# One Fourier-filter and gated-convolution kernel, one core: the hand-made planner gets a new order, laid out with a rule for eight transfers in flight

## The chip, the core and the metric

The kernel runs on one core of a Trainium2 chip. The time is that of one execution on the device, in microseconds (us); the kernel before takes 857.64 us (median of three runs, 857.32 to 858.21). One further execution was profiled; all views below are of that one.

## The reference

Everything is float32. A real Fourier transform along the sequence, a complex 256 x 256 matrix on the channels with a soft threshold, the transform back, and then a gated convolution:

```python
X = rfft(x, axis=1)                       # x: 8 batches x 3200 positions x 256 channels
Yr = Xr @ w_r - Xi @ w_i + b_r            # soft threshold, lam = 0.01, on Yr and on Yi
Yi = Xr @ w_i + Xi @ w_r + b_i
y = irfft(Yr + 1j * Yi, n=3200)
gate = sigmoid(causal_conv_5_taps(y, conv_w))
out = (gate * (y @ w_val)) @ w_out
```

## The kernel before, in words

The transform of length 3200 is split into 50 x 64, so that all of it is matrix products on TensorE (PE). A batch goes through three phases, and between them its data passes through DRAM, because the transform needs it turned round.

- **p1(b, u)**, u = 0 to 7: a tile of x (0.41 MB, four transfers, two of them of 48 rows and two of 2 rows; u = 0 has six) is loaded; PE multiplies it (L594, L599, L601) into a PSUM buffer of the tag ps_2, ACT copies one half out (L607) and VectorE (DVE) folds it twice (L613) into an SBUF tile s of the tag s1; then it is stored to a_dram (L554, and for u = 0 also four small transfers of L631).
- **p2(b, d)**, d = 0 to 6: a part of a_dram is loaded into a (two transfers, L650); PE does **s2** (L668, for d = 6 L660) into ps_2; ACT and DVE split the result into high and low parts xs (L709, L713, L716, L717, L720, L721). For each of its two units PE does **mixsum** (six matmuls, L786), DVE adds the bias (L788), and PE does **mix** (twelve matmuls, L782; the 13th unit is L772 and L773) into a buffer y_ps of which there are two, which ACT has seeded with the bias (L764). ACT and DVE make the threshold (L794, L796), PE does **s1i** (L737, last L731), ACT copies it out (L747) and it is stored to z_dram (L753).
- **p3(b, k)**, k = 0 to 7: zl is loaded from z_dram, PE does **s2i** (L848), ACT copies to y_sb (L852), DVE and ACT do the convolution and the sigmoid (L896, L899, L909), PE the two products v_ps and o_ps (L882, and L878 in the last blocks), DVE the gate (L933), ACT copies out (L958) and the result is stored (L960).

The tag ps_2 has three buffers, s1 two, x three, a two; batch 0's p1 borrows further SBUF tiles (tag by u: `("s1", "g_hl", "xs")[u % 3]`). A buffer is used again when its last reader is done, in the order in which pieces are emitted.

The weights w_val and w_out come as float64 words, and DVE turns each into float32 in thirteen instructions that stand behind each other in its row (L430, L436: the **conversion block**).

The order of all this is not left to a scheduler. The class `Plan` gets each piece with a due time `at`, an engine and a guessed duration, and `order()` plays them through: at each step it takes the engine whose next piece can begin first, and of the pieces that can begin within SLACK of that the one with the smallest due time. The kernel emits the instructions in that order, and each engine and each queue works its own row strictly in it. The due times are sums of the loop counters and of the table `O`. Transfers are nearly all issued from one queue, SP, in the planned order; the planner models them with one wire of `WIRE` bytes per ns, a completion time of `LANDED` ns, and a limit on the `BACKLOG`. Where it expects PE to stand still, it puts matmuls of zeros in (`fill`, L363 `zeros`).

Of the kernel before, what the change touches and what calls it, by code (L numbers as in the profile page):

```python
# [104 lines left out]
class Plan:  # L105
# [11 lines left out]
    def add(self, at, engine, busy, fn, uses=(), sets=(), new=None, delay=None, mode="r", kb=0, chain=None, extra=0):  # L117
        n = len(self.pieces)
        before = set()
        for key in uses:  # L120
            before |= set(self.writers.get(key, ()))
        for key in sets:
            before |= set(self.readers.get(key, ())) | set(self.writers.get(key, ()))
        for key in uses:
            self.readers.setdefault(key, []).append(n)
        for key in sets:
            self.writers[key], self.readers[key] = [n], []
        p = dict(n=n, at=at, engine=engine, busy=busy, fn=fn, before=before, new=new or {}, mode=mode, kb=kb, extra=extra,
                 tiles={key[:2] for key in (*uses, *sets)}, delay=busy + LAND[engine] if delay is None else delay)
        p["behind"] = {self.last[chain]} if chain in self.last else set()  # L130
        if chain:
            self.last[chain] = n
        self.pieces.append(p)
        return n

    def order(self):
        pieces = self.pieces
        for p in pieces:
            for tile_ in p["new"]:
                self.opened[tile_] = p["n"]  # L140
        users = {t: 0 for t in self.opened}
        after, follow = ([[] for _ in pieces] for _ in range(2))
        for p in pieces:
            opener = ({self.opened[t] for t in p["tiles"] if t in self.opened} | p["behind"]) - p["before"] - {p["n"]}
            for n in opener:
                follow[n].append(p["n"])
            p["left"] = len(p["before"]) + len(opener)
            p["ready"] = 0.0
            for n in p["before"]:
                after[n].append(p["n"])  # L150
            for t in p["tiles"]:
                if t in users:
                    users[t] += 1
        ends = {t: 0.0 for t in users}
        rows = {tag: [] for tag in self.slots}
        engines = sorted({p["engine"] for p in pieces})
        waiting = {e: [] for e in engines}
        for p in pieces:
            if not p["left"]:
                waiting[p["engine"]].append(p)  # L160
        free = {e: 0.0 for e in engines}
        mode, wire = "r", 0.0
        done = []

        def opens(p):
            at, ahead = 0.0, {}
            for tag in p["new"].values():
                row = rows[tag]
                n = len(row) + ahead.get(tag, 0)
                ahead[tag] = ahead.get(tag, 0) + 1  # L170
                if n >= self.slots[tag]:
                    old = row[n - self.slots[tag]]
                    if users[old]:
                        return None
                    at = max(at, ends[old])
            return at

        while len(done) < len(pieces):
            best = None
            for e in engines:  # L180
                could = []
                for p in waiting[e]:
                    at = opens(p)
                    if at is not None:
                        could.append((max(free[e], p["ready"], at, wire - BACKLOG if p["kb"] else 0.0), p))
                if not could:
                    continue
                first = min(c[0] for c in could)
                near = [c for c in could if c[0] <= first + SLACK[e]]

                lone = e == "PE" and sum(c[1]["mode"] == "q" for c in near) < 2
                start, p = min(near, key=lambda c: (c[1]["at"] + (0.0 if e != "PE" or c[1]["mode"] != "q" else -O["together"] if mode == "q"
                                                                   else O["hold"] if lone else 0.0), c[0]))
                if best is None or start < best[0]:
                    best = start, p
            assert best is not None, "no piece can begin"
            start, p = best
            e = p["engine"]
            waiting[e].remove(p)
            busy, delay = p["busy"], p["delay"]  # L200
            if e == "PE":
                slow = max([f for until, f in CLOCK if start < until], default=1.0)
                busy, delay = busy * slow, delay * slow
                to = SWITCH.get(mode + p["mode"], 0)
                busy, delay, mode = busy + to, delay + to, p["mode"]
            if p["kb"]:
                wire = max(wire, start + 800) + p["kb"] * 1024 / WIRE
                delay = wire - start + LANDED + p["extra"]
            free[e] = start + busy
            end = start + delay  # L210
            p["start"], p["end"], p["open"] = start, end, opens(p)
            done.append(p)
            for t, tag in p["new"].items():
                rows[tag].append(t)
            for t in p["tiles"]:
                if t in users:
                    users[t] -= 1
                    ends[t] = max(ends[t], end)
            for n, at in [(n, end) for n in after[p["n"]]] + [(n, start) for n in follow[p["n"]]]:
                q = pieces[n]  # L220
                q["left"] -= 1
                if q["engine"] == "PE" != e and at == end:
                    at += WEIGHTS
                q["ready"] = max(q["ready"], at)
                if not q["left"]:
                    waiting[q["engine"]].append(q)
        return done
# [42 lines left out]
WEIGHTS = 130  # L270
CLOCK = ((28000, 1.6), (45000, 1.2))
FILL = 36000, 200000
WIRE = 250
BACKLOG = 5000
LANDED = 2500


def dve(n, copy=False):
# [3 lines left out]
def act(n, kind="copy"):  # L282
# [6 lines left out]
NW = (NT - 1) * N1 + P  # L289
NG = NT // 2 * P + P  # L290
T = float(NU)
O = {'spread': -91.8948,
     'hold': 1.0724,
     'together': 1.2701,
     'later': -3.6572,
     'load_x': 9.9589,
     'p1': 0.1254,
     'p1_step': 1.2361,
     'load_a': -5.3199,
     's2': -1.7149,  # L300
     's1i': 1.553,
     'p3': 1.0966,
     'load_z': -28.9681,
     'y': 11.7985,
     'conv': 25.53,
     'val': 6.1049,
     'gate': -22.7084,
     'project': 7.8156,
     'late_val': 6.023,
     'late_out': 14.484,  # L310
     'turn': -55.8644,
     'pre': -4.984,
     'mix_sum': -1.4205,
     'p1_1': -7.3343,
     'load_x_1': -7.2435,
     'p1_2': -1.5627,
     'p3_0': 0.9988}
WARM = 2, 1, 1, 1, 8
SLOTS = {"x": 3, "zl": 3, "y_hl": 2, "s1": 2, "a": 2, "xs": 2, "sx": 1, "xz": 1, "tp": 3, "zst": 2,
         "acc": 2, "g_hl": 2, "o": 2, "ps_y": 2, "ps_2": 3, "a_dram": 2, "z_dram": 2}  # L320
# [6 lines left out]
def fourier_filter_then_gated_conv(ctx: ExitStack, tc: tile.TileContext, x, w_r, w_i, b_r, b_i,  # L327
# [5 lines left out]
    dram = ctx.enter_context(tc.tile_pool(name="dram", bufs=2, space=bass.MemoryType.DRAM))  # L333
    LATE_VAL, LATE_OUT = set(LATE[int(O["late_val"]):]), set(LATE[int(O["late_out"]):])
    plan = Plan(SLOTS)
    add = plan.add
# [214 lines left out]
    def by_rows(eng, out, in_, rows):  # L551

        for lo, hi in rows:
            eng.dma_start(out=out[lo:hi], in_=in_[lo:hi])  # L554
# [4 lines left out]
    STORED = []  # L559
# [4 lines left out]
    def p1(b, u, at):  # L564
# [8 lines left out]
        def load(h):  # L573
            xt = room(kx, x_tag, 4 * D) if h in (0, None) else tl[kx]
            src = x[b].rearrange("(n m) c -> n (m c)", m=N1)
            for g in range(NH) if h is None else (h,):
                eng = QUEUES[g][1] if early and u < BOTH else nc.sync
                lo = (N1 - 3 - 4 * u if g else 4 * u) * D
                n = 3 * D if g and u == 0 else 4 * D
                by_rows(eng, xt[half(g), 0:n], src[:, lo:lo + n], rows)  # L580
                if n < 4 * D:
                    by_rows(eng, xt[half(g), n:], src[:, NM * D:(NM + 1) * D], rows)
        if early:
            for h in range(NH):
                add(-100 + u, QUEUES[h][0] if u < BOTH else "SP", 650, lambda h=h: load(h), (), [kx + (h,)], None if h else {kx: x_tag}, kb=200)
        else:
            add(at + O["load_x"] + O["load_x_1"] * (b == 1), "SP", 1300, lambda: load(None), STORED if b == 1 else (),
                [kx + (0,), kx + (1,)], {kx: x_tag}, kb=400, chain="x")

        def products():  # L590
# [25 lines left out]
        busy = 2 * dve(D) if u == 0 else dve(512)  # L616
# [405 lines left out]
    for b in range(B):  # L1022
# [12 lines left out]
        start = (b + 1) * T + O["p3"] + O.get(f"p3_{b}", 0.0)  # L1035
# [40 lines left out]
```

## Time and profile before

| | |
|---|---|
| runs | 857.32, 857.64, 858.21 us |
| profiled execution | 859.73 us, of which the span from the first to the last instruction is 857.8 us |
| PE, matmuls | 821.0 us busy, 96% of the span, mean granted clock 0.973 |
| DVE | 736.2 us busy, 86% |
| ACT | 593.7 us busy, 69% |
| DMA | 162.27 MB, mean 189 GB/s |

Busy time of PE counts matmuls from start to end, and they overlap; a row of the timeline gives start, time taken, engine, line and tiles, and the distance from one row's start to the next is what a piece really costs PE. PEclk is the share of TensorE's clock that was granted. SPq is the queue that issues transfers: its rows are the issues, not the transfers.

### The profile page before, as it was taken

The numbers are of one execution on the slowest core, as the hardware profiler recorded it, in microseconds if no ns is written. First come the engines' busy times: TensorE is split into PE (matmuls) and PEld (weight loads), VectorE is DVE, ScalarE is ACT, GpSimd is POOL, SyncE is SP. The second block draws the span as 40 slices with busy tenths as digits, with TensorE's granted clock in tenths as the row PEclk, the third lists the DMA queues.
The fourth block names the chain that finished last, engine by engine and source line by source line (L and its number), as shares of the span: only waits on it lengthen the run. The fifth ranks groups of instructions, "written<-read, shape, count | busy, mean of one in ns | idle before, by whom it ended". The sixth has DMA issues, their size and how long they took to land.

```text
span 857.8 us, 23810 instructions
## 1 busy us (share of the span) xinstructions
PE 821.0 (96%) x9866; PEld 700.7 (82%) x9866; DVE 736.2 (86%) x1006; ACT 593.7 (69%) x903; POOL 4.5 (1%) x12
## 2 busy tenths in 40 slices
PE   8878867999999999999999999999999999999997
PEld 2456656889888988889988989899888999998874
DVE  3345679799998999899989998999989998998795
ACT  2234635778777786778777886878777787776753
POOL 0000000000000000000000000000001000000000
PEclk7888979999999999999999999999999999999999
DMA  6688889867886569776796759876895576225422
GB/s 169 182 190 224 246 214 250 228 179 191 209 234 185 165 180 258 203 204 174 224 245 195 192 175 248 206 206 187 231 234 158 157 200 193 71 83 173 133 76 96
DMA packets 125909, 162.27 MB, mean 189 GB/s; under 512 B 12528, under 2 KB 100234, under 8 KB 125802
## 3 DMA queue, kind: packets, MB, share of 16 engines
q1 hardware_dynamic: 125598, 160.34, 68.1%
q8 instruction: 78, 1.28, 0.7%
q10 hardware_dynamic: 204, 0.41, 0.2%
q14 instruction: 29, 0.24, 0.1%
HBM read 82.06 MB, written 78.64 MB: 187 GB/s over the span
## 4 chain that ended last, share of the span: by engine, by line
PE 69%; DVE 13%; DMA 9%; ACT 4%; SPq 3%; issue 2%; DVEq 0%; ACTq 0%
PE o_ps L882 13%; PE y_ps L782 12%; PE v_ps L882 11%; PE y_p L848 10%; PE y_ps L786 6%; DMA x<-in_x 4%; PE p L594 4%; PE s L668 4%; PE z_ps L737 4%; DVE acc L899 4%; PE v_ps L878 2%; SPq L554 2%; DMA zl<-z_dram 1%; DVE acc L933 1%; DVE gated L390 1%
## 5 line engine op out<-in xcount | busy, mean ns | idle before, releaser
L899 DVE SCALAR_TENSOR_TENSOR acc<-y_sb,cw_sb,acc 128x800 f32<-128x800 f32 x256 | 263.0, 1047 | 16.1 <-ACT acc L896 15.6
L782 PEld LDWEIGHTS y_ps<-w_sb,xs 128*128 128x128 f32 x1152 | 144.3, 191 | 28.4 <-DVE y_ps L788 12.4
L782 PE MATMUL y_ps<-w_sb,xs 128*128 128x256 f32 x1152 | 156.3, 286 | 11.1 <-DVE y_ps L788 11.0
L882 PE MATMUL o_ps<-gated,wo_sb 128*128 128x400 f32 x744 | 150.8, 349 | 0.8 <-DVE gated L390 0.8
L882 PEld LDWEIGHTS o_ps<-gated,wo_sb 128*128 128x128 f32 x744 | 134.6, 188 | 4.1 <-DVE gated L390 1.1
L882 PE MATMUL v_ps<-y_hl,wv_sb 128*128 128x400 f32 x648 | 128.4, 346 | 0.5 <-DVE s L613 0.5
L882 PEld LDWEIGHTS v_ps<-y_hl,wv_sb 128*128 128x128 f32 x648 | 115.4, 188 | 1.1 <-PE y_ps L786 0.7
L613 DVE TENSOR_TENSOR s<-p,s 128x512 f32<-128x512 f32 (+2 forms) x144 | 89.3, 626 | 27.5 <-ACT s L607 16.4
L848 PEld LDWEIGHTS y_p<-g_sb,zl 100*64 100x64 f32 x2048 | 89.1, 137 | 11.7 <-ACT y_ps L764 3.5
L848 PE MATMUL y_p<-g_sb,zl 100*64 100x100 f32 x2048 | 97.4, 251 | 0.7 <-DMA zl<-z_dram 0.5
L786 PE MATMUL y_ps<-w_sb,xs 128*128 128x256 f32 x576 | 90.0, 293 | 7.6 <-ACT y_ps L764 7.6
L786 PEld LDWEIGHTS y_ps<-w_sb,xs 128*128 128x128 f32 x576 | 79.3, 194 | 20.9 <-ACT y_ps L764 9.0
L794 ACT ACTIVATE tp<-y_ps,nlam 128x512 f32<-128x512 f32 (+1 forms) x104 | 70.0, 674 | 25.1 <-PE y_ps L782 25.1
L388 ACT CAST gated<-acc 128x800 fp32r<-128x800 f32 x62 | 53.3, 859 | 30.7 <-DVE acc L933 30.5
L601 PE MATMUL p<-x,f_sb 50*64 50x512 f32 x240 | 72.2, 654 | 1.7 <-DMA x<-in_x 1.7
L933 DVE TENSOR_TENSOR acc<-v_ps,acc 128x800 f32<-128x800 f32 x64 | 62.9, 984 | 11.4 <-PE v_ps L878 5.5
L796 DVE SCALAR_TENSOR_TENSOR tp<-y_ps,tp 128x512 f32<-128x512 f32 (+1 forms) x104 | 68.6, 661 | 4.1 <-ACT tp L794 4.0
L594 PE MATMUL p<-x,f_sb 50*64 50x512 f32 x256 | 71.6, 647 | 0.1
L668 PEld LDWEIGHTS s<-f_sb,a 64*64 64x64 f32 x3072 | 53.7, 137 | 19.5 <-issue 11.6
L909 ACT ACTIVATE acc<-acc 128x800 f32<-128x800 f32 x64 | 55.8, 878 | 16.3 <-DVE acc L899 16.0
L958 ACT COPY o<-o_ps 128x800 f32<-128x800 f32 x63 | 51.8, 822 | 21.3 <-PE o_ps L882 15.8
L716 DVE TENSOR_TENSOR sx<-s,sx 128x512 f32<-128x512 f32 x48 | 33.0, 688 | 38.2 <-ACT xs L713 37.2
(92 smaller groups left out, 1031.3 us busy)
## 6 DMA issues: line engine op xcount, KB each, us to landing
out<-o SPq DMA_DIRECT2D x126, 200.0 KB
a<-a_dram SPq DMA_DIRECT2D x96, 256.0 KB
z_dram<-z_t SPq DMA_DIRECT2D x48, 512.0 KB
zl<-z_dram SPq DMA_DIRECT2D x64, 384.0 KB
a_dram<-s SPq DMA_DIRECT2D x120, 192.0 KB
x<-in_x SPq DMA_DIRECT2D x119, 192.0 KB
a_dram<-s SPq DMA_DIRECT2D x120, 8.0 KB
x<-in_x SPq DMA_DIRECT2D x119, 8.0 KB
```

The lines of the kernel that those rows point to most:

```text
L594: nc.tensor.matmul(p[k * HP:(k + 1) * HP, 0, :], f1_sb[half(0), 0:HP], xt[half(0), k * 512:(k + 1) * 512], start=True, stop=True)
L601: nc.tensor.matmul(dst, f1_sb[half(1), 0:HP], back[:, 2 * k:2 * k + 2, :], start=True, stop=True)
L613: nc.vector.tensor_tensor(out=st()[lo:hi, h, n], in0=tl[kp][lo:hi, 0, n], in1=st()[lo:hi, 1, n], op=(ALU.add, ALU.subtract)[h])
L668: nc.tensor.matmul(p[e * HP:(e + 1) * HP, h, c, t, :], tl[ka][rows, t, c * P + e * HP:c * P + (e + 1) * HP], f2_sb[rows, (4 * d + t) * N1: ...
L782: nc.tensor.matmul(p[:, 1 - r, :], xm(hx, c, r, i), w_sb[:, m, hw, c, :], start=False, stop=k == 5, skip_group_check=True)
L786: nc.tensor.matmul(tl[ky][:, 0], sm(hx, c, i), w_sb[:, 0, hw, c, :], start=False, stop=k == 5, skip_group_check=True)
L794: nc.scalar.activation(out=buffer(kt, "tp", [P, 2, D])[:, 0:n], in_=tl[ky][:, 0:n], func=AF.Relu, bias=nlam)
L796: add(at + 0.2, "DVE", dve(n * D), lambda: nc.vector.scalar_tensor_tensor(out=tl[kt][:, 0:n], in0=tl[ky][:, 0:n], scalar=LAM, in1=tl[kt][: ...
L848: nc.tensor.matmul(dst[e * HP:(e + 1) * HP], zt[0:Q, m, c * P + e * HP:c * P + (e + 1) * HP], g, start=True, stop=True)
L882: nc.tensor.matmul(p[:, e, 0:TB], w[:, hw, c, e * P:(e + 1) * P], src(hy, c), start=n == 0, stop=n == 5)
L899: nc.vector.scalar_tensor_tensor(out=acc(c), in0=wide(c, j), scalar=cw_sb[:, c, j:j + 1], in1=acc(c), op0=ALU.mult, op1=ALU.add)
L933: add(at + O["gate"], "DVE", dve(2 * TB), lambda: nc.vector.tensor_tensor(out=part(), in0=by_half(tl[kv][:, :, 0:TB]), in1=part(), op=ALU. ...
```

## The change

The planner's model gets one more rule: it keeps the landing times of the last eight transfers of each of two groups (those issued from POOL, and the others), and a transfer may not begin before the eighth one ahead of it has landed. `WIRE` goes from 250 to 260 and `LANDED` from 2500 to 2200, all values of `O` are new, and the first x tiles of batch 1 no longer wait until batch 0's p1 results are stored (`STORED`). No tile, no instruction's shape and no number of buffers changes; PE's real matmuls are the same in number. Only the filling zeros go from 26 to 71 instructions. `SOFT` is set and used nowhere.

```diff
+        lanes, turn = {e: [0.0] * 8 for e in (False, True)}, {False: 0, True: 0}
+        def lane(p):
+            row, at = lanes[p["engine"] == "POOL"], turn[p["engine"] == "POOL"]
+            return max([row[(at + j) % 8] - 350 * j for j in range(lanes_of(p))], default=0.0)
...
-                        could.append((max(free[e], p["ready"], at, wire - BACKLOG if p["kb"] else 0.0), p))
+                        could.append((max(free[e], p["ready"], at, max(wire - BACKLOG, lane(p)) if p["kb"] else 0.0), p))
...
+                n = lanes_of(p)
+                for j in range(n):
+                    lanes[e == "POOL"][turn[e == "POOL"] % 8] = start + delay - p["kb"] * 1024 / WIRE * (n - 1 - j) / n
+                    turn[e == "POOL"] += 1
...
-WIRE = 250
+WIRE = 260
-LANDED = 2500
+LANDED = 2200
+def lanes_of(p):
+    return max(1, round(p["busy"] / (520 if p["engine"] == "POOL" else 360))) if p["kb"] else 0
...
-     'load_x': 9.9589,
+     'load_x': 40.9418,
...
-     'load_x_1': -7.2435,
+     'load_x_1': -69.2562,
...
-            add(at + O["load_x"] + O["load_x_1"] * (b == 1), "SP", 1300, lambda: load(None), STORED if b == 1 else (),
+            add(at + O["load_x"] + O["load_x_1"] * (b == 1), "SP", 1300, lambda: load(None), (),
```

In the changed kernel every line of the body stands 14 lines lower (L668 is L682 and so on); the text keeps the numbers of before.

**SP, where batch 0's second phase begins.** Before, the first parts of a (L650) are loaded right behind batch 0's last store (s_254), and batch 1's x follows between them:

```order
L554 DMA a_dram<-s_254 48x2x512
L554 DMA a_dram<-s_254 2x2x512
L490 DMA g_sb<-in_g 128x256
L650 DMA a<-a_dram 64x4x256 x2
L554 DMA x<-in_x 48x1024
L554 DMA x<-in_x 2x1024
L554 DMA x<-in_x 48x768
```

In the changed kernel three x tiles of batch 1 stand ahead of batch 0's stores and two more behind them, and only then come the loads of a, for d = 0 and d = 1 together (L664):

```order
L568 DMA x<-in_x 48x1024
L568 DMA x<-in_x 2x1024
L504 DMA g_sb<-in_g 128x256
L499 DMA f_sb<-in_f 128x256
L664 DMA a<-a_dram 64x4x256 x4
L568 DMA x<-in_x 48x1024
L568 DMA x<-in_x 2x1024
```

The first load of a moves from the 73rd transfer of this queue, with 6.98 MB ahead of it, to the 96th, with 9.16 MB ahead. Behind it now stand batch 1's last three x tiles (twelve transfers), and only then the stores of batch 1's first p1 results (s_306, s_337, s_408); a for d = 2 comes behind those.

**PE, at the first s2 (s_317 before, s_461 now).** Before:

```order
L987 MATMUL warm<-idle 128x512 x8
L363 MATMUL s_317<-zero_sb 128x128 x15
L668 MATMUL s_317<-f_sb,a 64x64 x32
L594 MATMUL p_374<-x,f_sb 64x512 x2
L599 MATMUL p_374<-x,f_sb 64x256 x2
L601 MATMUL p_374<-x,f_sb 64x512
L363 MATMUL p_396<-zero_sb 128x128 x9
```

Now (p_355 and p_380 are p1 of batch 1, u = 3 and 4):

```order
L608 MATMUL p_355<-x,f_sb 64x512 x2
L615 MATMUL p_355<-x,f_sb 64x512 x2
L377 MATMUL y_ps<-zero_sb 128x128 x2
L608 MATMUL p_380<-x,f_sb 64x512 x2
L615 MATMUL p_380<-x,f_sb 64x512 x2
L377 MATMUL y_ps<-zero_sb 128x128 x49
L682 MATMUL s_461<-f_sb,a 64x64 x32
L377 MATMUL y_ps<-zero_sb 128x128 x8
L682 MATMUL s_520<-f_sb,a 64x64 x32
```

Thirteen p1 pieces stand ahead of the first s2 where eight stood, and 49 zeros directly ahead of it.

**DVE and PE, at the first conversion block.** On DVE the block (st_894 is the loaded w_val, st_1086 the result) stood behind four folds of a p1:

```order
L788 TENSOR_TENSOR y_ps<-y_ps,bias_sb 128x256
L613 TENSOR_TENSOR s_1064<-p_1042,s_1064 128x256
L613 TENSOR_TENSOR s_1064<-p_1042,s_1064 64x256
L613 TENSOR_TENSOR s_1064<-p_1042,s_1064 128x256
L613 TENSOR_TENSOR s_1064<-p_1042,s_1064 64x256
L430 TENSOR_SCALAR st_1086<-st_894 128x512
```

It now stands behind the 11th bias addition and two small pieces of the 13th unit:

```order
L802 TENSOR_TENSOR y_ps<-y_ps,bias_sb 128x256
L710 CAST xz<-xs 128x512
L711 MEMSET xz 128x8
L444 TENSOR_SCALAR st_1161<-st_1030 128x512
L444 TENSOR_SCALAR st_1161<-st_1161 128x512 x3
```

PE, at the matmuls that wait for the bias addition behind the block: before, the mixsum (L786) of that unit is followed at once by its mix (L782):

```order
L599 MATMUL p_1042<-x,f_sb 64x256 x2
L601 MATMUL p_1042<-x,f_sb 64x512
L782 MATMUL y_ps<-w_sb,xs 128x256 x12
L786 MATMUL y_ps<-w_sb,xs 128x256 x6
L782 MATMUL y_ps<-w_sb,xs 128x256 x12
```

Now another mix and a whole s2 stand between them:

```order
L751 MATMUL z_ps<-tp,g_sb 64x256 x8
L800 MATMUL y_ps<-w_sb,xs 128x256 x6
L796 MATMUL y_ps<-w_sb,xs 128x256 x12
L682 MATMUL s_1185<-f_sb,a 64x64 x32
L796 MATMUL y_ps<-w_sb,xs 128x256 x12
```

More of the change, by code (lines that the diff above doesn't have):

```diff
@@ L272 @@
 FILL = 36000, 200000
-WIRE = 250
+WIRE = 260
 BACKLOG = 5000
-LANDED = 2500
+LANDED = 2200
+SOFT = 1500
+def lanes_of(p):
+    return max(1, round(p["busy"] / (520 if p["engine"] == "POOL" else 360))) if p["kb"] else 0
 def dve(n, copy=False):
@@ L291 @@
 T = float(NU)
[L292 to L295, printed above, removed]
-     'load_x': 9.9589,
[L297 to L308, printed above, removed]
+O = {'spread': -86.7866,
+     'hold': 0.9457,
+     'together': 1.3242,
+     'later': 3.7239,
+     'load_x': 40.9418,
+     'p1': -3.5894,
+     'p1_step': 1.5365,
+     'load_a': 23.6096,
+     's2': -1.5367,
+     's1i': 0.9416,
+     'p3': 7.1139,
+     'load_z': -8.9038,
+     'y': 3.7564,
+     'conv': 75.8192,
+     'val': 4.1041,
+     'gate': -19.9155,
+     'project': 5.84,
      'late_val': 6.023,
      'late_out': 14.484,
[L311 to L314, printed above, removed]
-     'load_x_1': -7.2435,
-     'p1_2': -1.5627,
-     'p3_0': 0.9988}
+     'turn': -33.3683,
+     'pre': -59.4674,
+     'mix_sum': -1.3262,
+     'p1_1': 1.8084,
+     'load_x_1': -69.2562,
+     'p1_2': 1.7884,
+     'p3_0': -1.6866}
 WARM = 2, 1, 1, 1, 8
```

## The prediction

> **What bounds the kernel now.** I read the stretches first (start and end in us; busy time and count of PE, of its weight loads, of DVE, ACT and POOL; granted clock, DMA share, GB/s), to see where PE loses time at all.
>
> ```profile
> 20.00:40.00 20.00, 20.00 (x83) 10.02 (x82) 9.19 (x15) 5.72 (x11) 0.00 (x0) 0.85 0.72 197
> 40.00:60.00 20.00, 15.01 (x208) 10.77 (x208) 7.06 (x13) 5.54 (x10) 0.00 (x0) 0.83 0.84 186
> 180.00:220.00 40.00, 40.00 (x496) 36.01 (x494) 38.03 (x54) 30.00 (x48) 0.00 (x0) 1.00 0.58 158
> 220.00:260.00 40.00, 38.39 (x512) 34.30 (x512) 39.56 (x52) 30.67 (x48) 0.00 (x0) 1.00 0.88 229
> 420.00:460.00 40.00, 40.00 (x557) 35.33 (x559) 35.66 (x47) 29.42 (x46) 0.00 (x0) 1.00 0.86 234
> 780.00:820.00 40.00, 39.83 (x376) 32.58 (x375) 32.46 (x35) 23.86 (x33) 0.00 (x0) 1.00 0.50 147
> ```
>
> From 180 to 820 us PE stands still for hardly 2 us, at full clock. In that stretch no order can win anything: it can only add switches or waits. What an order can change lies ahead of 180 us. The waits of PE up to 180 us (who, for whom, total, times, longest), and one of those after it, which lies in the last blocks:
>
> ```profile
> PE y_ps L782 <- DVE y_ps L788: 11.0, 3, 7.6
> PE y_ps L786 <- ACT y_ps L764: 6.6, 3, 4.5
> PE s L668 <- DMA a<-a_dram: 5.0, 2, 4.2
> PE s L668 <- DMA f_sb<-in_f: 2.5, 1, 2.5
> ...
> PE o_ps L882 <- DVE gated L390: 0.8, 1, 0.8
> ```
>
> So the question is how much PE work is done when the first s2i begins, and when that is. Pieces of PE cost, start to start where nothing waits:
>
> ```profile
> 160.53 0.95 PE L786 MATMUL y_ps<-w_sb,xs 128*128 128x256 f32 x6
> 161.32 1.52 PE L782 MATMUL y_ps<-w_sb,xs 128*128 128x256 f32 x12
> 162.77 0.65 PE L594 MATMUL p<-x,f_sb 50*64 50x512 f32 x2
> ...
> 163.68 1.11 PE L668 MATMUL s<-f_sb,a 64*64 64x64 f32 x64
> 164.73 1.59 PE L848 MATMUL y_p<-g_sb,zl 100*64 100x100 f32 x32
> ...
> 171.46 1.10 PE L737 MATMUL z_ps<-tp,g_sb 64*64 64x256 f32 x16
> 172.38 0.60 PE L594 MATMUL p<-x,f_sb 50*64 50x512 f32 x2
> ...
> 173.35 0.98 PE L786 MATMUL y_ps<-w_sb,xs 128*128 128x256 f32 x6
> ```
>
> That is 0.79 for mixsum, 1.45 for mix, 0.91 for p1, 1.05 for s2, 0.92 for s1i.
>
> **The start before.** The queue's own rows, and PE at the first s2 and the first s2i:
>
> ```profile
> 1.56 16.09 SPq L554 DMA_DIRECT2D x<-in_x  x28
> 17.92 0.22 SPq L496 DMA_DIRECT2D b_sb<-in_b_r  x1
> 18.64 1.53 SPq L554 DMA_DIRECT2D a_dram<-s  x4
> 20.27 2.86 SPq L631 DMA_DIRECT2D a_dram<-s  x4
> 26.42 11.80 SPq L554 DMA_DIRECT2D a_dram<-s  x24
> 40.99 1.33 SPq L650 DMA_DIRECT2D a<-a_dram  x2
> 47.01 3.69 SPq L554 DMA_DIRECT2D x<-in_x  x8
> ```
> ```profile
> 37.56 3.37 DMA a_dram<-s
> ```
> ```profile
> 44.76 0.48 PE L668 MATMUL s<-f_sb,a 64*64 64x64 f32 x4 [4.20 <-DMA a<-a_dram]
> ```
> ```profile
> 152.77 1.59 PE L848 MATMUL y_p<-g_sb,zl 100*64 100x100 f32 x32
> ```
>
> The first row shows the rule that the planner is given: 28 issues take 16.09 us, 0.57 each, where four stores take 0.38 each (1.53 for 4), because the queue stops until earlier transfers have landed. The 24 stores take 0.49 each.
>
> From 44.76 to 152.77, 108.0 us, the order puts 13 p1, 10 s2, 17 mixsum, 16 mix, 8 s1i and the small 13th unit (2.3): 11.8 + 10.5 + 13.4 + 23.2 + 7.4 + 2.3 = 68.6 us of PE. So 39.4 us are lost there: about 21 in waits (11.0 + 6.6 + 2.5 and 0.8 of the waits for a), and of the rest, by my estimate, about 13 in a lower clock and in zeros and about 5 that I can't name.
>
> **The change, part by part.**
>
> *The first s2 comes later.* SP in the changed kernel: as before to 18.4. The two weight matrices and f, then three x tiles of batch 1 (14 issues at 0.57): 1.5 + 8.0, to 27.9. Batch 0's stores: 1.5 + 2.9 + 28 x 0.49, to 46.0. Two x tiles 3.7, two constants 0.7, four loads of a 3.2: 53.6; a's data is there some 4 us after its issue, at about 54. But the first s2 now needs a ps_2 buffer of p1(1,2). Its copy goes into an s1 buffer, and s1 has two: it must wait until s of p1(1,0) is stored. That store stands behind twelve more x issues (5.5 at 0.46, the x8 row's rate) and takes 4.4 to 6.4: 63.5 to 65.5. Landing takes 3.37 by the row of the last store, then 0.6 for ACT's copy and 1.4 for two folds. So the first s2 begins at about 69.0 (bounds 65, with all issues at 0.40, and 72, with everything at 0.57). It is 24 us later, with five p1 (4.6 us) more behind it.
>
> The DMA page of the Trainium skill ("DMA: Bandwidth & Descriptors", Anatomy of one DMA) gives a fixed cost of about 2.0 us a transfer, measured on the other issuing path. With it instead of 3.37 the first s2 would come 1.4 us earlier; I keep the row, which holds transfer and queueing here.
>
> *The zeros* directly ahead of it cost nothing: 98 passes at about 0.12 are 11.5 us, between p1(1,4) at about 53 and 69. If a were ready at 54, they would cost 11.5.
>
> *From there to the first s2i* PE has 7 p1, 9 s2, 16 mixsum, 16 mix, 7 s1i and the 13th unit: 6.4 + 9.5 + 12.6 + 23.2 + 6.4 + 2.3 = 60.4. Of the 68.6 before, 3.7 (one each of p1, s2, mixsum and s1i) is done later now, the rest of the difference earlier. So the change breaks even here if the first s2i begins at 152.77 - 3.7 = 149.1, that is with 149.1 - 69.0 - 60.4 = 19.7 us lost instead of 39.4. What I find lost:
>
> The second s2 must wait for the second fold of p1(1,3), which DVE does behind the first piece of the first s2; then mixsum waits for the split: about 2.8.
>
> The conversion block, on DVE and on PE before:
>
> ```profile
> 108.92 2.15 DVE L430 TENSOR_SCALAR st<-st 128x512 int32<-128x512 int32 x5
> 115.01 0.69 DVE L436 TENSOR_TENSOR st<-st 128x512 f32<-128x512 f32 x1
> 115.73 0.43 DVE L788 TENSOR_TENSOR y_ps<-y_ps,bias_sb 128x256 f32<-128x256 f32 x1
> ```
> ```profile
> 107.71 0.86 PE L786 MATMUL y_ps<-w_sb,xs 128*128 128x256 f32 x6
> 116.22 2.93 PE L782 MATMUL y_ps<-w_sb,xs 128*128 128x256 f32 x12 [7.65 <-DVE y_ps L788]
> ```
>
> The block takes 6.8 us, and PE stood 7.65 since its mix came straight behind the mixsum. Now a mix and an s2 (2.5) lie between, and DVE has two pieces of 0.4 in all ahead of the block: 0.4 + 6.8 + 0.5 - 2.5, about 5. The second block had cost 4.5 (row L786 on L764 above); in the new order there is about 4.6 of PE work beside 9.2 of DVE's (the block, parts of two splits, a threshold): 4.6.
>
> The clock falls behind such a stop:
>
> ```profile
> 70.00:75.00 5.00, 4.86 (x23) 2.40 (x17) 1.92 (x3) 2.12 (x3) 0.00 (x0) 0.53 0.82 179
> 115.00:120.00 5.00, 3.78 (x17) 3.78 (x18) 3.14 (x7) 2.10 (x4) 0.00 (x0) 0.50 0.84 197
> 140.00:145.00 5.00, 2.47 (x11) 2.47 (x12) 4.73 (x9) 1.86 (x4) 0.00 (x0) 0.69 0.89 235
> ```
>
> The mix at 116.22 took 2.93 where one takes 1.52. I take 1.8 us for each of the two stops, 3.6 in all, and nothing for the stop at the first s2, which zeros cover.
>
> The clock gate of the Trainium skill ("TensorE: Matmul & The Clock Gate", Part 1) halves the clock after an idle window of about 3.4 us, and so lets a shorter stop go free. The 2.5 us wait for f (first list) is followed by 0.53 at 70 to 75, which speaks against that. By the rule the sum keeps its 3.6; by the row a stop of 2 to 3 us between the zeros and the first s2 adds up to 3.8.
>
> For shorter waits I take 1.5: the other bias waits (11.0 - 7.65 = 3.4) came where mix followed mixsum at once, which the new order does not do up to the block. And 3.5 for what I could not name before, cut by the shorter stretch. Sum: 2.8 + 5.0 + 4.6 + 3.6 + 1.5 + 3.5 = 21.0, between 14.5 (no unnamed loss, cheap clock) and 30 (as much lost per us as before). That is 1.3 more than the 19.7 to break even.
>
> *After it.* The stalls of 1 to 2 us between 219 and 246 (DVE at 39.56 of 40) can go, since by my count of DVE work to the gates the new order leaves DVE some 2 us more room there: -1.0, between -1.6 and +2. PE's changes between matmuls of 64 x 64 and of 128 x 128 weights rise from 169 to 177. A p1 with such a change behind it took 0.97 (172.38 to 173.35), one without 0.91; at 0.1 a change, an estimate, that is +0.8, between +0.4 and +1.2. The last blocks: PE work after the last s2i falls from 37.5 to 34.8, DVE gates stand as close as before, and the one wait there is 0.8: 0, between -0.8 and +1.5. In the steady part mix stands at least 1.4 us of PE work behind its mixsum (1.7 before), and the bias needs 0.43 plus what queues on DVE: nothing.
>
> **Sum.** +1.3 - 1.0 + 0.8 = +1.1 us on the profiled execution. That one's 859.73 (span 857.8 and 1.9 around it) stands 2.1 above the median of the runs; on the median the sum gives 858.7, and I say 858.5.
>
> **Rivals.** (1) *Not won back, slower.* In the new order a for d = 2 to 6 stands in SP behind stores which wait for DVE folds (s_408, s_498, s_558, s_610). By my times a lands 3.5 to 8 us ahead of its s2; if SP comes more than 5 us later, two of the five loads are exposed with 3.8 each (40.99 to 44.76) and a clock drop of about 1 each: +9.5, about 867. For it: the queue took 0.57 an issue in its full stretch; against it: from 69 us PE, not DMA, paces that loop.
> (2) *Faster.* SP issues at 0.40 where it isn't held up, so the first s2 comes at 65 (-4), and the unnamed loss goes (-3.5): about 850. For it: the stretch 20 to 40 ran at a DMA share of only 0.72, and x loads now fill it.
> (3) *The zeros bind.* If a's path needs no s1 buffer, PE works 49 zeros with the data there, +5 to +11, about 866. Against it: the buffer count above.
> (4) *The order does nothing measurable*: it is the middle of the likeliest case, since the new model only moves work ahead of 180 us.
>
> **Numbers.** The likeliest, 0.48: won back to within a few us, 853 to 862. Rival 1 0.24, rival 2 0.20, rival 3 0.05, else 0.03. A measurement can tell about 0.2%, 1.7 us, from no change. Of the likeliest a third is within that (0.17), 0.13 below, 0.18 above. Faster: 0.13 + 0.20 + 0.02 = 0.35; same: 0.20 with edges; slower: 0.45. The range for 8 in 10 runs from rival 2's 850 to rival 1's 867: 849 to 868.
>
> **What would show it.** In the changed profile: PE's first L682 at 65 to 72 with the zeros up to it; PE's wait on L802 at the first block near 5 instead of 7.65; the first L862 near 150 (before 148 the start is won, after 155 rival 1 holds); PE without gaps from about 190 on. If L682 starts at 55 to 61, right behind the zeros, the buffer argument is wrong. If gaps appear after 250 us, the claim that the rest is untouched is wrong.

## The result, and the profile after

The changed kernel takes 864.33 us (median of 863.11, 863.53, 865.12 and 866.27) against 857.84 for the one before: a ratio of 1.0078, 95% interval 1.0057 to 1.0100, so 6.5 us slower. The forecast was 858.5, with 853 to 862 as the likeliest case and a range from 849 to 868. The profiled execution took 863.11 (span 861.3), 3.4 more than the profiled one of before (859.73, span 857.8): part of the 6.5 is not in these two profiles, and that had to be explained too.

SP's own rows of the changed kernel, where the first s2 is decided (start, us, issues):

```profile
48.88 2.66 SPq L664 DMA_DIRECT2D a<-a_dram  x4
51.64 9.14 SPq L568 DMA_DIRECT2D x<-in_x  x12
60.91 1.39 SPq L568 DMA_DIRECT2D a_dram<-s  x4
62.41 2.89 SPq L645 DMA_DIRECT2D a_dram<-s  x4
```

ACT's row of the copy of p1(1,2), and PE's of the zeros and the first two s2:

```profile
66.95 0.59 ACT L621 COPY s<-p 128x512 f32<-128x512 f32 x1 [20.94 <-DMA a_dram<-s]
```
```profile
52.84 11.21 PE L377 MATMUL y_ps<-zero_sb 128*128 128x128 f32 x98
69.09 1.98 PE L682 MATMUL s<-f_sb,a 64*64 64x64 f32 x64 [5.04 <-issue]
74.05 1.16 PE L682 MATMUL s<-f_sb,a 64*64 64x64 f32 x64 [0.38 <-ACT xs L734]
```

The twelve x issues take 9.14 us. What the queue itself waited for between 48 and 66 us (total, times, longest):

```profile
SPq L568 <- DMA a<-a_dram: 4.4, 4, 1.6
```

So 4.4 of the 9.14 are four x issues that wait until the four loads of a, eight transfers ahead of each, have landed: the rule of eight that the planner was given holds at just this place. The issues of the store of p1(1,0) end at 65.30, and 1.65 later ACT's copy begins, which had stood still for 20.94 us: the s1 buffer of the prediction. Two folds on, at 69.09, comes the first s2. It takes 1.98 where one takes 1.05, behind a stop of PE: the zeros ended at 64.05, and PE then stood for 5.04.

PE at the two conversion blocks, the first s2i, and the last product:

```profile
122.67 2.93 PE L796 MATMUL y_ps<-w_sb,xs 128*128 128x256 f32 x12 [4.60 <-DVE y_ps L802]
...
142.42 0.98 PE L800 MATMUL y_ps<-w_sb,xs 128*128 128x256 f32 x6 [3.45 <-ACT y_ps L778]
...
150.60 4.34 PE L862 MATMUL y_p<-g_sb,zl 100*64 100x100 f32 x96
...
850.88 5.54 PE L892 MATMUL o_ps<-acc,w_late 128*128 128x400 f32 x16
```

The same last product before:

```profile
847.61 5.54 PE L878 MATMUL o_ps<-acc,w_late 128*128 128x400 f32 x16
```

What PE waits for after 180 us, and two of the stretches that were shown of before:

```profile
PE o_ps L896 <- DVE xs L731: 0.5, 1, 0.5
PE p L608 <- DVE xs L731: 0.3, 1, 0.3
PE y_p L862 <- DMA zl<-z_dram: 0.2, 1, 0.2
```
```profile
220.00:260.00 40.00, 39.65 (x534) 35.38 (x534) 38.97 (x53) 31.33 (x48) 0.00 (x0) 1.00 0.86 237
...
780.00:820.00 40.00, 40.00 (x358) 33.87 (x358) 39.93 (x44) 26.30 (x35) 0.00 (x0) 1.00 0.42 129
```

After 180 us PE's waits are 1.0 in all, against 3.2 before (1.0, 0.8, 0.5, 0.5, 0.2, 0.2 in the same view). PE stands still even less than before, and yet the changed kernel loses there. From the first s2i to the last product it takes 850.88 - 150.60 = 700.28 us, before 847.61 - 152.77 = 694.84. Of these 5.4 us more, 3.7 are the p1, s2, mixsum and s1i that are done later now; +1.7 are lost.

### The profile page after: what moved, and what is told of

It reads as the page before. It is cut to its first block, busy times and chain, and to the rows that moved or that the text cites. A ratio compares the mean times of both kernels' runs of the same rounds, so it can differ in the third digit from the quotient of the medians.

```text
span 861.3 us, 24023 instructions
## 1 busy us (share of the span) xinstructions
PE 831.7 (97%) x9956; PEld 708.0 (82%) x9956; DVE 736.0 (85%) x1006; ACT 596.5 (69%) x903; POOL 5.2 (1%) x12
## 4 chain that ended last, share of the span: by engine, by line
PE 82%; DMA 6%; DVE 5%; ACT 2%; SPq 2%; issue 2%; ACTq 0%; DVEq 0%
PE o_ps L896 15%; PE y_ps L796 14%; PE v_ps L896 13%; PE y_p L862 10%; PE y_ps L800 8%; PE s L682 5%; PE p L608 5%; PE z_ps L751 4%; DMA x<-in_x 4%; PE v_ps L892 3%; DVE acc L913 1%; DMA a_dram<-s 1%; SPq L568 1%; SPq L645 1%; PE p L615 1%
## 5 line engine op out<-in xcount | busy, mean ns | idle before, releaser
L796 PE MATMUL y_ps<-w_sb,xs 128*128 128x256 f32 x1152 | 154.8, 285 | 4.6 <-DVE y_ps L802 4.6
L796 PEld LDWEIGHTS y_ps<-w_sb,xs 128*128 128x128 f32 x1152 | 143.2, 190 | 19.0 <-issue 9.3
L862 PE MATMUL y_p<-g_sb,zl 100*64 100x100 f32 x2048 | 100.7, 252 | 0.2 <-DMA zl<-z_dram 0.2
L800 PE MATMUL y_ps<-w_sb,xs 128*128 128x256 f32 x576 | 87.2, 288 | 5.7 <-ACT y_ps L778 5.7
L800 PEld LDWEIGHTS y_ps<-w_sb,xs 128*128 128x128 f32 x576 | 77.1, 189 | 18.5 <-ACT y_ps L778 8.1
L621 ACT COPY s<-p 128x512 f32<-128x512 f32 x64 | 37.7, 588 | 61.3 <-DMA a_dram<-s 37.0
L608 PE MATMUL p<-x,f_sb 50*64 50x512 f32 x256 | 73.0, 653 | 5.3 <-issue 3.5
L615 PE MATMUL p<-x,f_sb 50*64 50x512 f32 x240 | 72.9, 652 | 0.2 <-DMA x<-in_x 0.2
L682 PEld LDWEIGHTS s<-f_sb,a 64*64 64x64 f32 x3072 | 52.0, 136 | 19.9 <-issue 12.0
L778 ACT COPY y_ps<-bias_sb 128x256 f32<-128x256 f32 x104 | 39.3, 379 | 37.2 <-DVE tp L810 36.2
L402 ACT CAST y_hl<-y_sb 128x800 fp32r<-128x800 f32 x54 | 46.4, 860 | 24.8 <-PE v_ps L896 24.6
```

Of the source, the lines that this page charges most:

```text
L402: nc.scalar.copy(out=high(), in_=src())
L608: nc.tensor.matmul(p[k * HP:(k + 1) * HP, 0, :], f1_sb[half(0), 0:HP], xt[half(0), k * 512:(k + 1) * 512], start=True, stop=True)
L615: nc.tensor.matmul(dst, f1_sb[half(1), 0:HP], back[:, 2 * k:2 * k + 2, :], start=True, stop=True)
L682: nc.tensor.matmul(p[e * HP:(e + 1) * HP, h, c, t, :], tl[ka][rows, t, c * P + e * HP:c * P + (e + 1) * HP], f2_sb[rows, (4 * d + t) * N1: ...
L796: nc.tensor.matmul(p[:, 1 - r, :], xm(hx, c, r, i), w_sb[:, m, hw, c, :], start=False, stop=k == 5, skip_group_check=True)
L800: nc.tensor.matmul(tl[ky][:, 0], sm(hx, c, i), w_sb[:, 0, hw, c, :], start=False, stop=k == 5, skip_group_check=True)
```

## The experiments

Each kernel with its time against runs of the kernel before on the same chip (first s2i and last product from the one profiled execution of each; line numbers differ from kernel to kernel):

| kernel | median us | ratio, 95% interval | first s2i | last product |
|---|---|---|---|---|
| e1 old start, new rest | 871.07 | 1.0154 (1.0135 to 1.0173) | 150.66 | 858.18 |
| e2 new start, old rest | 869.77 | 1.0137 (1.0119 to 1.0154) | 152.37 | 856.94 |
| e3 one store ahead of x | 863.82 | 1.0066 (1.0049 to 1.0082) | 150.97 | 850.93 |
| e4 two stores ahead of x | 860.98 | 1.0041 (1.0024 to 1.0058) | 147.58 | 848.36 |
| e5 e4, fewer changes of kind | 876.82 | 1.0233 (1.0219 to 1.0248) | 148.10 | 864.62 |
| e6 new rule, old table | 868.98 | 1.0140 (1.0124 to 1.0155) | 154.68 | 857.13 |
| e7 e4 without those zeros | 859.49 | 1.0032 (1.0021 to 1.0044) | 147.95 | 848.62 |
| e8 before, fewer changes of kind | 889.35 | 1.0379 (1.0364 to 1.0393) | 152.25 | 877.54 |
| e9 e7, s2i and p1 woven | 883.77 | 1.0303 (1.0283 to 1.0323) | 148.23 | 871.04 |
| e10 before, f early | 857.69 | 1.0002 (0.9987 to 1.0016) | 151.13 | 845.15 |
| e11 e10, DVE's urgent pieces first | 859.77 | 1.0018 (1.0006 to 1.0030) | 153.49 | 847.67 |
| e12 the changed kernel again | 864.62 | 1.0096 (1.0079 to 1.0113) | 152.00 | 852.22 |

They ran in four groups, each on another chip (e1 to e4, e5 to e8, e9 to e11, e12), where the kernel before took 858.06, 857.23, 858.26 and 857.29: medians of two groups can be compared to about 1 us, the ratios more closely.

**Is it the start or the rest?** e1 and e2 change from one set of rules and due times to the other at 180 us of planned time. In e1 FIRST is 0, the old side, as printed here; in e2 it is 1.

```diff
+CUT = 180000
+FIRST = 0
...
+def side(t):
+    return FIRST if t < CUT else 1 - FIRST
...
+                v = side(free[e])
...
+                start, p = min(near, key=lambda c: (due(c[1], v) + (0.0 if e != "PE" or c[1]["mode"] != "q" else -O["together"].v[v] if mode == "q"
+                                                                   else O["hold"].v[v] if lone else 0.0), c[0]))
```

> Order made by the old rule, old table and old x dependency up to 180 us of planned time, by the new ones after it (the first 196 rows of PE are those of before, the last 686 those of the changed kernel). Theory S (the start costs most of the +6.5): 857.5 to 860, first s2 near 44.8, first s2i near 152.8. Rival R (the steady part costs most): 861 to 864, with more waits of PE after 180 us than before.

> The other way round: new order up to 180 us of planned time (the first 170 rows of PE are those of the changed kernel), old rule and table after it. Theory S: 862 to 865, since the late first s2 (69) and what follows stay. Rival R: 858 to 861, only the +1.5 to +2 that the profile shows at the first s2i stay.

Both missed, on both theories: each mixture is some 5 to 7 us slower than the worse of its parents. In e1 PE waits for DVE behind the seam, and its clock falls there (the two largest waits of PE from 180 to 300 us: total, times, longest; and one stretch):

```profile
PE p L668 <- DVE s L687: 2.7, 1, 2.7
PE v_ps L956 <- DVE s L687: 2.2, 1, 2.2
```
```profile
210.00:220.00 10.00, 8.95 (x110) 7.80 (x102) 7.37 (x11) 4.68 (x9) 0.00 (x0) 0.73 0.79 209
```

My reading is that an order is laid out for what its own start has left undone; in any case the two halves can't be priced by exchanging them. For e2 the waits shown after 180 us are 3.5 in all and don't carry its loss; where the rest went stayed open. The two are used below only for their starts, which are row by row those of their parents.

**The late first s2.** In e3 and e4 the stores are moved in the changed kernel's list, and nothing else: PE, DVE and ACT keep their rows.

```diff
         done = self.order()
+        first, moved = MOVED[0], MOVED[1:]
+        at = next(i for i, p in enumerate(done) if p["n"] == first)
+        up = [p for p in done[:at] if p["n"] in moved]
+        done = [p for p in done[:at] if p["n"] not in moved] + [done[at]] + up + done[at + 1:]
```

`MOVED[0]` is the store of p1(1,0) in e3 and that of p1(1,1) in e4, which has the first one ahead of it already; the others are the x tiles of p1(1,5), (1,6) and (1,7).

> Changed kernel, all of PE, DVE and ACT in the same order; in SP's row only the store of batch 1's first p1 result stands ahead of the twelve x issues instead of behind them. By the buffer theory the copy of ACT that waited for that store (66.95) comes at about 57.8, the first s2 directly behind the zeros at 64.1 instead of 69.1, the second s2 at about 71.6 instead of 74.05 (it waits for the next store); time 861 to 863.5. Rival (a's data is the late one, or all comes back later): first s2 at 69, or first s2i at 150.6 as now; 863 to 866.

> As the kernel before it in this set, with the stores of the first two p1 results of batch 1 ahead of the twelve x issues. By the buffer theory the first s2 at 64.1 and the second at 67 to 69 instead of 74.05, where zeros (two lots) are what it stands behind; first s2i 2 to 5 us earlier (145.6 to 148.6), time 859 to 862.5. Rival (the next a, or x, is late in its place): first s2i within 1 us of 150.6, time 863 to 866.

ACT's copy that stood at 66.95, and the next of its kind, in e3:

```profile
60.49 0.59 ACT L628 COPY s<-p 128x512 f32<-128x512 f32 x1 [13.36 <-DMA a_dram<-s]
68.80 0.58 ACT L628 COPY s<-p 128x512 f32<-128x512 f32 x1 [7.72 <-DMA a_dram<-s]
```

PE's first two s2 and the first s2i, in e3 and then in e4:

```profile
65.18 1.16 PE L691 MATMUL s<-f_sb,a 64*64 64x64 f32 x64
72.22 1.31 PE L691 MATMUL s<-f_sb,a 64*64 64x64 f32 x64 [3.90 <-ACT xs L743]
...
150.97 4.34 PE L871 MATMUL y_p<-g_sb,zl 100*64 100x100 f32 x96
```
```profile
63.21 1.16 PE L691 MATMUL s<-f_sb,a 64*64 64x64 f32 x64
67.36 1.16 PE L691 MATMUL s<-f_sb,a 64*64 64x64 f32 x64 [1.01 <-ACT xs L743]
...
147.58 4.34 PE L871 MATMUL y_p<-g_sb,zl 100*64 100x100 f32 x96
```

In e3 the first s2 comes 3.9 us earlier, as the buffer theory has it; but the next copy waits for the next store (68.80), the second s2 for that copy's folds, and the first s2i is where it was: all of it comes back at the next wait of the same kind, as the second half of the rival had it. With both stores ahead (e4) the second s2 comes 6.7 us earlier, the first s2i 3.0, and the time falls by 3.3 to 860.98. So the wait for these two stores is shown as what made the second phase late.

**The zeros.** e7 is e4 without the 49 and the 8 zeros.

```diff
     def fill(t, n):
+        if n == 49 or n == 8:
+            return
```

> The kernel with two stores first (860.98), without the 49 and 8 zeros ahead of the first two s2. If zeros are what binds there, the first s2 comes at 60 to 61 instead of 63.2 and the time falls by up to 2 (859 to 860). If their price is only the clock that they keep up: the first s2 takes 2 us instead of 1.1, later pieces too, and the time stays within 1.5 of 861.

```profile
61.50 1.99 PE L691 MATMUL s<-f_sb,a 64*64 64x64 f32 x64 [8.70 <-DVE s L634]
66.46 1.99 PE L691 MATMUL s<-f_sb,a 64*64 64x64 f32 x64 [2.98 <-ACT xs L743]
...
147.95 4.34 PE L871 MATMUL y_p<-g_sb,zl 100*64 100x100 f32 x96
```

The first s2 comes 1.7 earlier, so the zeros did bind a little in e4, but both s2 take 1.99 and the first s2i is where it was. 859.49 against 860.98, of two groups and with overlapping intervals: no difference that can be told.

**The rule without the table.** e6 is the changed kernel with the old values of `O`.

```diff
-O = {'spread': -86.7866, ...
+O = {'spread': -91.8948, ...
```

> One part of the change: the rule of eight transfers, 260 and 2200 and x of batch 1 without its wait, with the old table of due times. Changes out of the four kinds 208, as before (207). Theory K: after 200 us no dearer than before (PE loses 1 to 2 us there besides its matmuls, the changed kernel 5); the start has 13 p1 ahead of the first s2 like the changed kernel, so first s2 at 60 to 70; time 857 to 861. Rival (the rule itself harms, in the start): 862 to 866.

A miss, above both ranges. The start is worse than in either parent: the first s2i comes at 154.68, and one mix fewer is done by then than in the changed kernel. At the first conversion block PE stands for 5.64, where it stands for 4.60 in the changed kernel and stood for 7.65 before; no matmul runs in this stretch (busy time of PE, its loads, DVE, ACT, POOL; clock, DMA share, GB/s):

```profile
120.00:125.00 5.00, 0.00 (x0) 0.00 (x0) 4.76 (x10) 0.01 (x1) 0.00 (x0) 0.88 0.90 220
```

That explains about 1 us against the changed kernel; where the other 3 or 4 that this start loses go stayed open. So the rule by itself is not what one would keep. What the new table does without the rule was not run.

**What the rest loses.** e5 and e8 give a bonus in the due time to a piece of p1, s2, s1i or s2i of the same kind as the last one on PE (`start_of` is true from 200 us of planned time on); e9 does the opposite by weaving halves of s2i and p1.

```diff
+                                                         - (1.5 if e == "PE" and c[1]["mode"] == "q" and start_of(c) and c[1]["fn"].__code__ is kind else 0.0), c[0]))
```
```diff
+                if p["n"] in pairs:
+                    for part in range(2):
+                        p["fn"](part)
+                        self.pieces[pairs[p["n"]]]["fn"](part)
+                    continue
```

> The kernel with two stores first (860.98), and from 200 us of planned time on a bonus of 1.5 in the due time for a piece of the same kind as PE's last one. PE's changes out of p1, s2, s1i and s2i into another kind fall from 231 to 180 (before: 207). Theory K (a change of kind costs 0.1 to 0.3 each, also between two kinds of 64-wide pieces, and that is what the steady part lost): 5 to 8 us less, 853 to 856. Rival (only the switches between 64-wide and 128-wide pieces cost, 94 to 86 of them at 0.1): 859.5 to 861, or more if the clumps make PE wait.

> The kernel before with the same bonus for a piece of the same kind after 200 us of planned time: 207 changes become 187. Its first 235 rows of PE are those of before, so its start should be that of before. Theory K: 2 to 4 us less than before, 854 to 856. Rival: within 1 us of before, or slower if the clumps make PE wait.

> The kernel without those zeros (859.49); 22 times after 200 us where PE does an s2i and then a p1, it does half of the s2i, half of the p1, and the other halves. DVE, ACT and SP keep their rows. 44 more changes of kind, none of them between 64-wide and 128-wide weights. Theory K, with prices fitted over the groups of all traces so far (0.151 for each group of s2i, 0.087 for each of p1): 22 x 0.238 = +5.2, so 863.5 to 866. Rival (only switches between widths cost): 859 to 861.

Theory K missed in all three, by 21, 33 and 18 us. For e5 and e8 the rivals had allowed for it: the clumps made PE wait. From the first s2i to the last product PE's idle time, added up over its records, is 14.9 us in e5 (1.6 in e4) and 24.1 in e8 (3.1 before). The two largest waits of many in e5:

```profile
PE y_ps L814 <- ACT y_ps L792: 4.5, 3, 1.7
PE v_ps L910 <- DVE acc L961: 1.9, 1, 1.9
```

So these two don't tell the price, only that it couldn't be saved in this way. (That three ps_2 buffers are too few to feed a row of equal pieces is a guess; no run has more.) Counted on PE's records after 200 us, moreover, e8's bonus hardly lowered what costs. What matters is the shape of tile a matmul uses, and there are three here, not two: 128 x 128 (mixsum, mix, v, o), 64 x 64 (p1, s2, s1i) and the 100 x 64 of s2i. Changes between the three after 200 us: before 170, changed kernel 199, e5 156 (e4 198), e8 168. The price, in the changed kernel's rows, an s2 with s2i behind it, an s2i with p1 behind it:

```profile
305.14 1.16 PE L682 MATMUL s<-f_sb,a 64*64 64x64 f32 x64
306.23 1.59 PE L862 MATMUL y_p<-g_sb,zl 100*64 100x100 f32 x32
307.75 0.65 PE L608 MATMUL p<-x,f_sb 50*64 50x512 f32 x2
```

and in e9 a woven pair, then an s2i, an s2 and a p1 left whole:

```profile
307.60 0.91 PE L917 MATMUL y_p<-g_sb,zl 100*64 100x100 f32 x16
308.44 1.08 PE L661 MATMUL p<-x,f_sb 50*64 50x512 f32 x4
309.44 0.91 PE L917 MATMUL y_p<-g_sb,zl 100*64 100x100 f32 x16
310.28 1.07 PE L668 MATMUL p<-x,f_sb 50*64 50x512 f32 x4
311.29 1.69 PE L851 MATMUL y_ps<-w_sb,xs 128*128 128x256 f32 x12
...
319.74 1.59 PE L917 MATMUL y_p<-g_sb,zl 100*64 100x100 f32 x32
321.26 1.16 PE L737 MATMUL s<-f_sb,a 64*64 64x64 f32 x64
322.24 0.60 PE L661 MATMUL p<-x,f_sb 50*64 50x512 f32 x2
322.26 0.60 PE L668 MATMUL p<-x,f_sb 50*64 50x512 f32 x2
```

An s2 before an s2i takes 306.23 - 305.14 = 1.09, before a p1 (the same shape) 322.24 - 321.26 = 0.98. Over all profiles after 200 us, the median distance from a piece's last matmul to the next piece is 0.519 us for p1 where the shape changes and 0.409 where it doesn't (314 and 206 cases), 0.306 and 0.196 for s1i, 0.148 and 0.038 for s2, 0.209 and 0.117 for mixsum and mix, 0.275 and 0.184 for the products v_ps and o_ps: 0.09 to 0.11 each. For s2i it is about 0.15: alone 307.75 - 306.23 = 1.52, three in a row before

```profile
329.72 4.34 PE L848 MATMUL y_p<-g_sb,zl 100*64 100x100 f32 x96
333.99 0.65 PE L594 MATMUL p<-x,f_sb 50*64 50x512 f32 x2
```

4.27, which is 0.29 under 3 x 1.52, for two changes. The Trainium skill ("TensorEngine Tiling (Array Packing)", Tiling Modes, Key Properties) says that a change of the tiling mode drains TensorE and one of the tile alone does not; these rows agree, and give its price.

e9 confirms the 0.15 for s2i (two halves 0.84 each, 0.16 over 1.52), and its time failed on something else: a p1 cut in halves takes 1.00 + 1.01 instead of about 1.0, since its two pairs of matmuls (in e9 L661 and L668, at 322.24 and 322.26 in a whole one) run at the same time; in the kernel they read different halves of the partitions. 22 x 1.0 + 22 x 0.16 = 25.5 is about what e9 lost against e7 (24.3 by the medians, 23.2 by the ratios).

**Could the kernel before be bettered in its start?** e10 issues the part of f that PE waited 2.46 us for ahead of an x tile and two stores; e11 also puts bias additions, thresholds and seeds ahead of, or inside, the conversion blocks.

```diff
+        f, a = (next(p for p in done if p["n"] == MARK[k]) for k in ("f2", "a"))
+        done.remove(f)
+        done.insert(done.index(a) + 1, f)
```
```diff
+HOIST = {"w_val": 3, "w_out": 4}
+SPOTS = {"w_val": (0, 0, 5), "w_out": (0, 3, 7, 8)}
```

Here `f` is part 2 of f_sb and `a` the load of a for d = 2; `HOIST` is how many of DVE's pieces go up in e11, `SPOTS` ahead of which of the thirteen instructions.

> The kernel before with one issue moved: the part of f that PE waited for at 66.46 to 68.92 is issued right behind the loads of a for d = 2, at about 53 instead of 63.8. The third s2 then begins at about 66.5 and the clock does not fall from 70 to 77 (p1 1.97, mix 2.67 there), 3 to 5 us won by 77. Theory A (PE's own work sets the pace up to the first conversion block): 852.5 to 855. Rival (DVE's block or a later load is what is late, and the gain is given back): 856 to 858.

> The kernel with f early, and at the two conversion blocks DVE does the bias additions and thresholds that PE waits for ahead of the block or inside it instead of behind it, and ACT the seeds ahead of the cast that waits for the block; PE and SP keep their rows. PE's waits of 7.65 and 4.5 fall to under 2 each. Theory P (PE's row has work that it can do meanwhile): 1 to 5 us less than the kernel with f early. Rival D (DVE is busy without a gap there, so PE only waits a little later): within 1 us of it.

e10: the wait for f is gone and the clock holds from 70 to 75 us (0.53 before), but in this execution PE stood 6.4 in its longest wait for a instead of 4.2 (a wait of PE, and the stretch):

```profile
PE s L676 <- DMA a<-a_dram: 7.0, 2, 6.4
```
```profile
70.00:75.00 5.00, 5.00 (x65) 3.23 (x66) 2.92 (x5) 2.32 (x4) 0.00 (x0) 1.00 0.86 213
```

857.69, no difference: not settled whether the gain is there and lost in the spread. e11: rival D in its mechanism, though its time is 2.1 above e10's and not within 1 (the intervals overlap). The longest wait for a bias addition fell from 7.65 to 2.4 and that for a seed from 4.5 to 2.3, and two others took their place:

```profile
119.27 0.48 PE L750 MATMUL s<-f_sb,a 64*64 64x64 f32 x4 [5.38 <-DVE st_cw L513]
...
146.51 1.99 PE L819 MATMUL z_ps<-tp,g_sb 64*64 64x256 f32 x16 [5.12 <-DVE s L693]
```

Both wait for DVE again: it is what is late in that stretch, and making PE wait less at one place only brought the wait at another.

**What the two profiles didn't show.**

> The changed kernel itself once more, for another profiled execution and more runs. Theory V (what the profile of one execution leaves open, +3.5 in spans against +6.5 between medians, is that the start differs by some 2 us from one execution to the next): first s2i between 150.5 and 152.5, median 863 to 866, and after 200 us every stretch within 0.3 of the first profile. Rival (the steady part differs between executions, or the first profile was typical): first s2i at 150.6 again, and the time above 863 is lost after 200 us.

The same order, executed again: first s2i and last product.

```profile
152.00 4.34 PE L862 MATMUL y_p<-g_sb,zl 100*64 100x100 f32 x96
...
852.22 5.54 PE L892 MATMUL o_ps<-acc,w_late 128*128 128x400 f32 x16
```

The first s2i is 1.40 later than in the first profile, the last product 1.34: the whole difference arises in the start, and what follows repeats to 0.06 us. Theory V holds. The first s2i with the old start was at 152.77, 152.25 and 150.66 (before, e8, e1), mean 151.9; with the new one at 150.60, 152.37 and 152.00 (changed, e2, e12), mean 151.7. With the 3.7 us of work put off, the new start is 3.5 later, not the 1.5 of the one pair; the three of each kind lie up to 2 apart, so this is good to about 1. The four executions with both stores moved (e4, e5, e7, e9) have the first s2i at 147.58 to 148.23, mean 148.0, and with the 3.7 that is 151.7, the old start's place. The two late stores are thereby shown as the cause of what the new start cost, and e4 and e7 stay 2.3 to 2.9 us above the kernel before by the rest.

## Why the prediction was right or wrong

The account, in us: start +3.5 (means of three executions each). From the first s2i to the last product: 694.84, 694.02 and 694.18 in the old order (before, e10, e11), 700.28, 700.22, 699.96, 700.78 and 700.67 in the new (changed, e12, e3, e4, e7): 6.0 more, less 3.7, +2.3. Behind the last product +0.2 (861.3 - 850.88 against 857.8 - 847.61). Sum +6.0, against +6.5 and +7.3 in the two comparisons; 0.5 to 1.3 stays open.

*The first s2 comes later.* 69.0 forecast, 69.09 measured (69.61 and 69.96 in e2 and e12), by the right cause (e3, e4). That it fits so closely is luck, since three errors cancel: SP was through with the loads of a at 51.54 instead of 53.6; the twelve x issues took 9.14 instead of 5.5, because four of them waited for those loads; and the store's data was there 1.65 after its last issue instead of 3.37. The row of 3.37 counts from an issue's start; in the same place, from the end of the last store's issue (38.22) to the landing at 40.93, it is 2.7. The sentence from the Trainium skill ("DMA: Bandwidth & Descriptors", Anatomy of one DMA: about 2.0, on another issuing path) was nearer than the row the prediction kept.

*The zeros* cost nothing: right, since PE stood 5.04 behind them. That they would cover the stop was wrong: the first s2 took 1.98 behind it, and with the second s2's wait some 4.4 were lost up to the first mixsum at 75.61 (6.5 for two s2 of 1.05), where the prediction had 2.8.

*From there to the first s2i.* 81.5 us in the first profile, of which 60.4 are PE's pieces: 21.1 lost, 21.0 forecast. The blocks: 5.0 forecast and 4.60 measured, 4.6 and 3.45 + 0.82. First s2i 149.1 + 1.3 = 150.4 forecast, 150.60 measured. What failed is the comparison, and on both sides: 152.77 is the latest of three executions of the old start (mean 151.9), and the 150.60 that the forecast met is the earliest of three of the new one (mean 151.7). The term of +1.3 is +3.5.

On the clock, the prediction kept the row (0.53 behind a stop of 2.46) against the rule of the Trainium skill ("TensorE: Matmul & The Clock Gate", Part 1) that a stop shorter than about 3.4 us goes free. The runs don't settle it. In e10, without that stop, the same stretch ran at 1.00, but so it did behind another one of nearly that length, which e10 still has:

```profile
66.01 0.98 PE L794 MATMUL y_ps<-w_sb,xs 128*128 128x256 f32 x6 [2.27 <-ACT y_ps L772]
```

*After it.* Stalls: -1.0 forecast; by PE's idle time from the first s2i to the last product (3.1, 2.6 and 2.7 in the old order, 1.2 to 1.8 in the new) they are -1.3. The changes between weights: +0.8 forecast, for 8 more at 0.1. The price was right and the count wrong, because it took the planner's two classes. By shape, after 200 us: 18 more changes out of s2i at 0.145, 13 more from 64 x 64 into s2i at 0.11, 4 more from 128 x 128 into it at 0.09, 6 fewer between the other two at about 0.1: 2.6 + 1.4 + 0.4 - 0.6 = +3.8. With the stalls +2.5, where +2.3 was measured. This is the mis-sized term of the rest: the new order does nearly every s2i alone where the old one had them in twos and threes. It also answers the prediction's first step, that no order can win anything where PE hardly stands still: these changes are part of PE's busy time, and the old order had 170 of them.

Two other orders test this sum. Without idle time and the work that is put off, e6 takes 1.1 us more than the old order between those two points, with 10 more changes, as it should. e2 takes 5.7 more with 23 more changes, which the price explains only to about half.

**Sum.** +1.1 forecast, +6.0 in the account: 2.2 more for the start, 3.0 more for the changes of shape, 0.3 less for the stalls and 0.2 behind the last product, which comes to 6.2. The place on the median was well taken (its own execution stands 2.1 above).

**Rivals.** The time lies above the likeliest case (853 to 862) and no rival's mechanism occurred; that the range held it is luck, since its upper end was rival 1's 867. (1) Its time came near, its mechanism did not occur: no s2 waits for a in the list of waits after. (2) The unnamed loss did not go. (3) The zeros didn't bind in the changed kernel. (4) 6.5 us is well clear of the 1.7 that the prediction called measurable. "PE without gaps" after 190 came true; it was no sign of a rest without loss.

## What to carry to other kernels

A list of waits doesn't hold what a change of tile shape costs on PE: count the changes by shape in both orders, and price them by the distance between pieces. A start that waits for transfers differed by up to 2 us between executions here, so a break-even taken from one profile is good to that and no better. And where a buffer is freed by a store, look at what stands ahead of that store in its queue; moving one store only uncovers the next (e3), moving both pays (e4).

## What the runs showed of the hardware

- A change among the three tile shapes cost PE 0.09 to 0.15 us, also between 64 x 64 and 100 x 64.
- p1's two pairs of matmuls run at the same time (322.24 and 322.26 in e9); apart they take 1.00 and 1.01 us instead of about 1.0 for both.
- SP took 0.76 us an issue for twelve x issues directly behind four loads of a (9.14, of which 4.4 were waits for these loads to land), and 0.40 to 0.47 where stores stood between (4.85 in e3, 5.32 in e7, 5.65 in e4).
- The same order, executed twice, repeated to 0.06 us over 700 us of the steady part and differed by 1.4 us in the first 150.
